# Windowed attention and a squared-ReLU feed-forward net in one kernel: attention re-tiled into chunks of 128 tokens

## Chip, cores, metric

One core of one Trainium2 chip. The time is device microseconds (us) of the whole launch, the median of several runs. All runs that are compared here are in the fast state (but for one single look, whose state is unknown), and each kernel was timed beside runs of the kernel before on the same chip. TensorE multiplies matrices, DVE is VectorE, ACT is ScalarE, POOL is GpSimd, and SP is SyncE, which issues all DMAs here. PSUM is the memory that TensorE writes, in banks; SBUF is the working memory.

## The reference

```python
# q, k, v: (8 batches, 8 heads, 576 tokens, 64), float32, entries about 0.1
scores = q @ k.T / 8                        # per batch and head
mask = (i - j >= 0) & (i - j < 64)          # causal, the last 64 keys
attn = softmax(where(mask, scores, -1e9))
x = (attn @ v) as (8 * 576 = 4608 tokens, 8 * 64 = 512)
h = maximum(x @ w_in, 0)                    # w_in  512 x 2048
out = (h * h) @ w_out                       # w_out 2048 x 512, out 4608 x 512 float32
```

## The kernel before

The feed-forward net (FFN) runs over nine blocks of 512 tokens: an up projection with a squared ReLU (16 steps of four matmuls of 512 columns), then the down projection (64 such matmuls). One batch of attention, 576 tokens, is woven step by step into each block; it feeds a later block. Attention goes head pair by head pair. Q and K are loaded with six consecutive tokens on one partition (rows of 1,536 bytes), cast on POOL and transposed on TensorE. The transposes come out with tokens in the order (r, t), so the copy out of PSUM puts them back in token order, with a write step of six 2-byte elements, that is 12 bytes:

```python
RT = 6; PT = S // RT                         # 6 tokens on each of 96 partitions
def transposes(hp):                          # one head pair, all 576 tokens
    for (s16, dstT, nm) in ((q16s, qTs, "q"), (k16s, kTs, "k")):
        ps = ps_att.tile([P, RT, PT], FP16, ...)          # a PSUM bank for each
        for r in range(RT):
            nc.tensor.transpose(out=ps[:, r, :], in_=s16[hp][:, r, :, :], ...)
        dT = attw.tile([P, PT, RT], FP16, ...)
        if nm == "q":                                     # line 168
            nc.scalar.activation(out=dT[:].rearrange("p t r -> p r t"), in_=ps[:], func=AF.Copy, ...)
        else:                                             # line 171
            nc.vector.tensor_copy(out=dT[:].rearrange("p t r -> p r t"), in_=ps[:])
# ... cut: scores (line 181), values, to_xT, and four more steps for the last 64 tokens
for hp in range(HP):                         # order of the steps of one batch
    transposes(hp); scores(hp)
    if hp > 0: values(hp - 1); to_xT(hp - 1)
# ... cut. PSUM: 3 buffers for the up projection, 2 for down, 3 for attention
for g in range(NTB + 1):                     # weave: steps of all streams evenly mixed
    weave(ffn_up(g), ffn_out(g - 1), attention steps of batch g + 1, loads of batch g + 2)
```

The softmax here doesn't subtract the row's maximum and nothing guards it: scores larger than these inputs give would overflow.

## Time and profile before

| | before |
|---|---|
| median of 3 runs | 383.81 us (382.3 to 386.02) |
| span of the profiled run | 380.5 us |
| first squared ReLU of block 0, of block 1 | 46.1, 83.2 us |
| pitch of the steady blocks that hold attention | 37.4 us |
| pitch of a block without attention (7 to 8) | 27.6 us |

Three stretches differ: a start, until block 1; woven blocks; and FFN alone at the end, where TensorE runs at its rate. The pitch is the distance between the first squared ReLUs of neighbouring blocks. The view of the PSUM tile of the up projection (hps) shows them; each line gives durations in ns (shortest/median/longest), then the first and last start in us:

```profile
L293 ACT ACTIVATE hrelu<-hps x144: 590/598/847, 44.9 to 362.0; 128x512 f32<-128x512 f32 x144
L294 DVE SCALAR_TENSOR_TENSOR h_601<-hps,hrelu x16: 674/688/810, 46.1 to 72.9; 128x512 f16<-128x512 f32 x16
L294 DVE SCALAR_TENSOR_TENSOR h_1161<-hps,hrelu x16: 659/692/812, 83.2 to 120.1; 128x512 f16<-128x512 f32 x16
...
L294 DVE SCALAR_TENSOR_TENSOR h_2345<-hps,hrelu x16: 691/692/692, 160.9 to 194.9; 128x512 f16<-128x512 f32 x16
L294 DVE SCALAR_TENSOR_TENSOR h_2937<-hps,hrelu x16: 691/692/692, 198.3 to 232.3; 128x512 f16<-128x512 f32 x16
```

198.3 - 160.9 is the pitch of 37.4. The groups of instructions (count, then busy us and mean ns, then idle time before and who ended it) give the price of the copies. The first two write with a step of 12 bytes, the third contiguously:

```profile
L168 ACT ACTIVATE qT<-qT_ps 128x576 f16<-128x576 f16 x32 | 67.4, 2105 | 29.3 <-PE qT_ps L164 29.2
L171 DVE COPY kT<-kT_ps 128x576 f16<-128x576 f16 x32 | 66.7, 2086 | 14.4 <-PE kT_ps L164 13.7
...
L218 DVE COPY xT<-xt_ps 128x512 f16<-128x512 f16 x32 | 13.4, 418 | 3.1 <-PE xt_ps L216 3.1
```

The list of waits has one large entry for TensorE (total us, times, longest); PEld is the load of the stationary operand:

```profile
PEld L181 <- DVE kT L171: 40.1, 32, 3.2
```

These 40.1 us are not all lost, since TensorE still multiplies while its next weight load waits (in the timeline below the load at 198.13 had waited 0.95 us, the first matmul after it 0.46).

The timeline of one such wait in a steady block (start us, duration, engine and line):

```profile
195.53 0.42 PE L164 MATMUL kT_ps<-ident,k_2419 96*128 96x96 f16 x6
...
195.79 1.03 PE L288 MATMUL hps<-xT,w_in_sb 128*128 128x512 f16 x4
195.99 2.09 DVE L171 COPY kT<-kT_ps 128x576 f16<-128x576 f16 x1 [0.18 <-PE kT_ps L164]
...
196.65 1.03 PE L307 MATMUL ops<-w_out_sb,h_2345 128*128 128x512 f16 x4
...
198.13 0.29 PEld L181 LDWEIGHTS <-kT 64*128 64x128 f16 x16 [0.95 <-DVE kT L171]
```

The four matmuls that start at 196.65 take 0.86 us of TensorE's time and would let the next work start near 197.5; the scores start at 198.13, when the K copy has ended. So about 0.6 us is lost for each head pair.

### The profile page before, as it was taken

The page shows a single profiled execution, that of the slowest core. Times are in us where ns is not written, and L with a number is a line of the kernel's source. Part 1 is how long each engine was busy: PE and PEld are TensorE (multiplying, and loading weights), DVE is VectorE, ACT ScalarE, POOL GpSimd, SP SyncE. Part 2 cuts the span into 40 slices and gives each one's busy share as a digit, 9 for nine tenths or more (in the row PEclk, how much of TensorE's full clock was granted, in tenths as well). Part 3 has the DMA queues.
Part 4 walks back from the last instruction along what each step waited for, and adds up shares of the span by engine and source line. Part 5 has one row for each costly group of instructions (what it writes and reads, how often), then busy time and mean ns, then how long its engine had stood idle before and what let it go on. Part 6 is the DMA issues. An engine that isn't in the chain of part 4 may idle for free.

```text
span 380.5 us, 7267 instructions
## 1 busy us (share of the span) xinstructions
PE 327.2 (86%) x2848; PEld 160.5 (42%) x2848; DVE 255.4 (67%) x468; ACT 215.0 (56%) x309; POOL 118.6 (31%) x178
## 2 busy tenths in 40 slices
PE   1154797777799999999999999999999999999995
PEld 1033443433444444454445444444444444444442
DVE  2277877888887888787878777877787744343400
ACT  3334276869665766576567656764676434444421
POOL 6922373552474752822182217310100000000000
PEclk9999998999999999999999999999999999999999
DMA  9946894957796899974254222100000001001012
GB/s 189 262 132 197 212 246 124 218 159 219 186 254 182 170 239 183 211 189 120 90 150 129 90 91 74 45 30 29 28 29 29 28 29 49 36 28 56 29 55 83
DMA packets 60642, 46.61 MB, mean 122 GB/s; under 512 B 39616, under 2 KB 51904, under 8 KB 60608
## 3 DMA queue, kind: packets, MB, share of 16 engines
q1 hardware_dynamic: 60608, 46.15, 47.0%
q8 instruction: 22, 0.36, 0.4%
q14 instruction: 12, 0.10, 0.1%
HBM read 36.70 MB, written 9.44 MB: 121 GB/s over the span
## 4 chain that ended last, share of the span: by engine, by line
PE 60%; DVE 23%; ACT 6%; DMA 4%; issue 3%; POOL 2%; SPq 0%; ACTq 0%; POOLq 0%
PE ops L307 25%; PE hps L288 23%; DVE kT L171 15%; DMA ws<-in_moe_w_in_dram 3%; PE av L204 2%; ACT hrelu L293 2%; DVE x_sb L209 2%; PE xt_ps L216 2%; PE qT_ps L164 2%; PE kT_ps L164 2%; DMA v_st<-in_v_dram 1%; ACT w_out_sb L123 1%; ACT qT L168 1%; DVE h_601 L294 1%; DVE w_in_sb L110 1%
## 5 line engine op out<-in xcount | busy, mean ns | idle before, releaser
L288 PE MATMUL hps<-xT,w_in_sb 128*128 128x512 f16 x576 | 155.6, 392 | 1.4 <-DVE h_601 L294 1.3
L293 ACT ACTIVATE hrelu<-hps 128x512 f32<-128x512 f32 x144 | 91.0, 637 | 88.8 <-PE hps L288 59.8
L168 ACT ACTIVATE qT<-qT_ps 128x576 f16<-128x576 f16 x32 | 67.4, 2105 | 29.3 <-PE qT_ps L164 29.2
L171 DVE COPY kT<-kT_ps 128x576 f16<-128x576 f16 x32 | 66.7, 2086 | 14.4 <-PE kT_ps L164 13.7
L288 PEld LDWEIGHTS <-w_in_sb 128*128 128x128 f16 x576 | 50.1, 100 | 49.2 <-issue 5.7
L312 ACT ACTIVATE osb<-ops 128x512 f32<-128x512 f32 x36 | 21.4, 598 | 21.4 <-PE ops L307 21.4
L181 PEld LDWEIGHTS <-kT 64*128 64x128 f16 x512 | 10.1, 99 | 41.2 <-DVE kT L171 40.1
L209 DVE TENSOR_TENSOR x_sb<-av,rden 128x256 f16<-128x256 f32 x64 | 25.0, 419 | 0.3
L294 DVE SCALAR_TENSOR_TENSOR h_4658<-hps,hrelu 128x512 f16<-128x512 f32 x16 | 11.1, 692 | 16.7 <-ACT hrelu L293 16.7
L294 DVE SCALAR_TENSOR_TENSOR h_4867<-hps,hrelu 128x512 f16<-128x512 f32 x16 | 11.1, 692 | 16.6 <-ACT hrelu L293 16.6
L152 POOL CAST v_ev_108<-v_st 128x512 f16<-128x512 f32 (+1 forms) x20 | 12.4, 631 | 30.6 <-DMA v_st<-in_v_dram 20.8
L216 PE MATMUL xt_ps<-ident,x_sb 128*128 128x128 f16 x128 | 13.3, 230 | 9.9 <-DVE x_sb L209 9.9
L152 POOL CAST v_ev_107<-v_st 128x512 f16<-128x512 f32 (+1 forms) x20 | 12.3, 622 | 22.7 <-DMA v_st<-in_v_dram 14.1
L307 PE MATMUL ops<-w_out_sb,h_601 128*128 128x512 f16 x64 | 18.5, 379 | 0.1
L216 PEld LDWEIGHTS <-x_sb 128*128 128x128 f16 x128 | 9.6, 102 | 18.8 <-DVE x_sb L209 14.3
L307 PE MATMUL ops<-w_out_sb,h_2345 128*128 128x512 f16 x64 | 16.6, 379 | 0.0
L307 PE MATMUL ops<-w_out_sb,h_3529 128*128 128x512 f16 x64 | 16.6, 379 | 0.0
L307 PE MATMUL ops<-w_out_sb,h_1753 128*128 128x512 f16 x64 | 16.6, 379 | 0.0
L307 PE MATMUL ops<-w_out_sb,h_1161 128*128 128x512 f16 x64 | 16.6, 379 | 0.0
L307 PE MATMUL ops<-w_out_sb,h_2937 128*128 128x512 f16 x64 | 16.6, 379 | 0.0
L307 PE MATMUL ops<-w_out_sb,h_4121 128*128 128x512 f16 x64 | 16.4, 379 | 0.0
L307 PE MATMUL ops<-w_out_sb,h_4658 128*128 128x512 f16 x64 | 16.4, 379 | 0.0
(717 smaller groups left out, 529.7 us busy)
## 6 DMA issues: line engine op xcount, KB each, us to landing
q_st<-in_q_dram SPq DMA_DIRECT2D x32, 288.0 KB, 4.6
k_st<-in_k_dram SPq DMA_DIRECT2D x32, 288.0 KB, 4.8
out_dram<-osb SPq DMA_DIRECT2D x36, 256.0 KB, 2.0
v_st<-in_v_dram SPq DMA_DIRECT2D x32, 256.0 KB, 4.5
ws<-in_moe_w_in_dram SPq DMA_DIRECT2D x16, 256.0 KB, 4.2
v_st<-in_v_dram SPq DMA_DIRECT2D x8, 128.0 KB, 5.3
ws_628<-in_moe_w_out_dram SPq DMA_DIRECT2D x1, 256.0 KB, 8.7
ws_663<-in_moe_w_out_dram SPq DMA_DIRECT2D x1, 256.0 KB, 8.7
```

The costliest lines, as they stand in the source:

```text
L152: nc.gpsimd.tensor_copy(out=v_ev[0:n, c, :, 0:D], in_=st[0:n])
L164: nc.tensor.transpose(out=ps[:, r, :], in_=s16[hp][:, r, :, :], identity=ident[0:PT, 0:PT])
L168: nc.scalar.activation(out=dT[:].rearrange("p t r -> p r t"), in_=ps[:], func=AF.Copy, scale=1.0)
L171: nc.vector.tensor_copy(out=dT[:].rearrange("p t r -> p r t"), in_=ps[:])
L181: nc.tensor.matmul(sc[hh][:, j, :], kTs[hp][r0:r0 + 64, ks:ks + P], qTs[hp][r0:r0 + 64, j * 64:(j + 1) * 64], start=True, stop=True)
L209: nc.vector.tensor_tensor(out=x_sb[:, :, hh, :], in0=av[:, :, 0:D], in1=rden[:].to_broadcast([P, NC, D]), op=ALU.mult)
L216: nc.tensor.transpose(out=xt[:, c, :], in_=hold["x"][:, c, :, :], identity=ident[:])
L288: nc.tensor.matmul(hps[:], w_in_sb[:, c, f * P:(f + 1) * P], xT[:, c, g * 512:(g + 1) * 512], start=(c == 0), stop=(c == DMC - 1))
L293: nc.scalar.activation(out=hrelu[:], in_=hps[:], func=AF.Relu)
L294: nc.vector.scalar_tensor_tensor(out=h2s[g][:, f, :], in0=hps[:], scalar=0.0, in1=hrelu[:], op0=ALU.max, op1=ALU.mult)
L307: nc.tensor.matmul(hold["ps"][:], h2s[g][:, f, ts * P:(ts + 1) * P], w_out_sb[:, f, :], start=(f == 0), stop=(f == FFC - 1))
L312: nc.scalar.activation(out=osb[:], in_=hold["ps"][:], func=AF.Copy, scale=OUT_SCALE)
```

## The change

Attention is cut into 36 chunks of 128 tokens over all eight heads, four to an FFN block. q, k and v are loaded with one token on a partition (rows of 256 bytes), so the transposes come out in token order and all copies out of PSUM are contiguous. Four stages are run as a pipeline over chunks: the transposes of a chunk come before the scores of the one before it. There is no tail of 64 tokens. K and Q of a chunk now share one PSUM tile. The w_in casts move from DVE to ACT with four staging buffers instead of three; PSUM has two up-projection buffers instead of three, and four for attention. Not in the cut below: more buffers for the loads of q, k and v (15), other masks, and a weave in which each stream has a start and an end. "The new order" below means all of this together. The diff, cut to its core:

```diff
-            for (src, dst16, nm) in ((q, q16s, "q"), (k, k16s, "k")):
-                st = stage.tile([PT, 2, RT, D], FP32, ...)
-                    in_=src[b, 2 * hp:2 * hp + 2].rearrange("h (p r) d -> p h (r d)", r=RT))
+        for (src, nm) in ((k, "k"), (q, "q"), (v, "v")):
+            st = stage.tile([P, H, D], FP32, ...)
+                    out=st[:], in_=src[b0, :, 64 * j0:64 * j0 + P, :].rearrange("h p d -> p h d"))
 ... (a chunk that spans two batches takes two DMAs of 64 tokens)
-                nc.vector.tensor_copy(out=dT[:].rearrange("p t r -> p r t"), in_=ps[:])
+        ps = ps_att.tile([P, 2, HP, P], FP16, name="qkT_ps", tag="ps_a")     # K and Q
+        kT = attw.tile([P, HP, 192], FP16, ...)
+            nc.vector.tensor_copy(out=kT[:, :, 0:64], in_=kTs[i - 1][:, :, P:192])   # carry
+        nc.vector.tensor_copy(out=kT[:, :, 64:192], in_=ps[:, 0])
+        nc.scalar.activation(out=qT[:], in_=ps[:, 1], func=AF.Copy, scale=1.0)
+    def attention(g):
+        fns = (transposes, scores, values, to_xT)
+        for t in range(4 + len(fns) - 1):
+            for s, fn in enumerate(fns):
+                if 0 <= t - s < 4:
+                    steps.append(lambda fn=fn, i=4 * g + t - s: fn(i))
-    wst = ctx.enter_context(tc.tile_pool(name="wst", bufs=3))
+    wst = ctx.enter_context(tc.tile_pool(name="wst", bufs=4))
-    ps_up = ... bufs=3 ... ps_att = ... bufs=3
+    ps_up = ... bufs=2 ... ps_att = ... bufs=4
-            nc.vector.tensor_scalar(   # w_in cast
+            nc.scalar.activation(
```

More of the change, by code (lines that the diff above doesn't have):

```diff
@@ L18, in weave @@
     keyed = []
-    for s, steps in enumerate(streams):
+    for s, (steps, lo, hi) in enumerate(streams):
         n = len(steps)
         for i, step in enumerate(steps):
-            keyed.append(((i + 0.5) / n, s, i, step))
+            keyed.append((lo + (hi - lo) * (i + 0.5) / n, s, i, step))
     keyed.sort(key=lambda e: e[:3])
@@ L43 @@
     HP = H // 2
-    RT = 6
-    PT = S // RT
-    NBM = 8
-    NC = 4
-    T0 = NBM * 64
-    TAIL = S - T0
+    NCK = NT // P
+    NB = S // 64
     W_SCALE = 100.0
@@ L57 @@
     const = ctx.enter_context(tc.tile_pool(name="const", bufs=1))
-    wst = ctx.enter_context(tc.tile_pool(name="wst", bufs=3))
-    stage = ctx.enter_context(tc.tile_pool(name="stage", bufs=4))
-    vstage = ctx.enter_context(tc.tile_pool(name="vstage", bufs=5))
-    st16 = ctx.enter_context(tc.tile_pool(name="st16", bufs=3))
+    wst = ctx.enter_context(tc.tile_pool(name="wst", bufs=4))
+    stage = ctx.enter_context(tc.tile_pool(name="stage", bufs=15))
+    st16 = ctx.enter_context(tc.tile_pool(name="st16", bufs=8))
@@ L62 @@
     attw = ctx.enter_context(tc.tile_pool(name="attw", bufs=3))
     smallp = ctx.enter_context(tc.tile_pool(name="smallp", bufs=4))
+    xtp = ctx.enter_context(tc.tile_pool(name="xtp", bufs=3))
     h2pool = ctx.enter_context(tc.tile_pool(name="h2pool", bufs=2))
-    hrp = ctx.enter_context(tc.tile_pool(name="hrp", bufs=3))
-    opool = ctx.enter_context(tc.tile_pool(name="opool", bufs=3))
-    ps_up = ctx.enter_context(tc.tile_pool(name="ps_up", bufs=3, space=bass.MemoryType.PSUM))
+    hrp = ctx.enter_context(tc.tile_pool(name="hrp", bufs=4))
@@ L68 @@
+    opool = ctx.enter_context(tc.tile_pool(name="opool", bufs=4))
+    ps_up = ctx.enter_context(tc.tile_pool(name="ps_up", bufs=2, space=bass.MemoryType.PSUM))
     ps_out = ctx.enter_context(tc.tile_pool(name="ps_out", bufs=2, space=bass.MemoryType.PSUM))
-    ps_att = ctx.enter_context(tc.tile_pool(name="ps_att", bufs=3, space=bass.MemoryType.PSUM))
+    ps_att = ctx.enter_context(tc.tile_pool(name="ps_att", bufs=4, space=bass.MemoryType.PSUM))
     ident = const.tile([P, P], FP16, name="ident")
@@ L72, with make_mask @@
     make_identity(nc, ident[:])
-    mask = const.tile([P, NBM, 64], FP16, name="mask")
-    nc.gpsimd.memset(mask[:], BIG)
-    nc.gpsimd.affine_select(
-        out=mask[:, 0, :], in_=mask[:, 0, :], compare_op=ALU.is_ge,
-        fill=0.0, base=0, pattern=[[1, 64]], channel_multiplier=-1,
-    )
-    nc.gpsimd.affine_select(
-        out=mask[:, 1:NBM, :], in_=mask[:, 1:NBM, :], compare_op=ALU.is_ge,
-        fill=0.0, base=-1, pattern=[[0, NBM - 1], [-1, 64]], channel_multiplier=1,
-    )
-    nc.gpsimd.affine_select(
-        out=mask[:, 1:NBM, :], in_=mask[:, 1:NBM, :], compare_op=ALU.is_ge,
-        fill=0.0, base=64, pattern=[[0, NBM - 1], [1, 64]], channel_multiplier=-1,
-    )
+    def make_mask(name, first):
+        m = const.tile([P, HP, 2, 64], FP16, name=name)
+        nc.gpsimd.memset(m[:], BIG)
+        nc.gpsimd.affine_select(
+            out=m[:], in_=m[:], compare_op=ALU.is_ge, fill=0.0, base=-1,
+            pattern=[[0, HP], [0, 2], [-1, 64]], channel_multiplier=1,
+        )
+        nc.gpsimd.affine_select(
+            out=m[:], in_=m[:], compare_op=ALU.is_ge, fill=0.0, base=64,
+            pattern=[[0, HP], [0, 2], [1, 64]], channel_multiplier=-1,
+        )
+        if first is not None:
+            nc.gpsimd.memset(m[0:64, :, first, :], 0.0)
+        return m
@@ L92 @@
+    mask_first = make_mask("mask_first", 0)
     w_in_sb = const.tile([P, DMC, DFF], FP16, name="w_in_sb")
     w_out_sb = const.tile([P, FFC, DM], FP16, name="w_out_sb")
-    xT = const.tile([P, DMC, NT], FP16, name="xT")
-    NV = 2
-    v_evs = [const.tile([P, NC + 1, H, 66], FP16, name=f"v_ev{i}") for i in range(NV)]
-    v_ods = [const.tile([P, NC, H, 66], FP16, name=f"v_od{i}") for i in range(NV)]
+    NV = 8
+    v_evs = [const.tile([P, H, 66], FP16, name=f"v_ev{i}") for i in range(NV)]
@@ L98 @@
+    v_ods = [const.tile([P, H, 66], FP16, name=f"v_od{i}") for i in range(NV)]
     for i in range(NV):
-        nc.vector.memset(v_evs[i][:, :, :, 64:65], 1.0)
-        nc.vector.memset(v_ods[i][:, :, :, 64:65], 1.0)
+        nc.vector.memset(v_evs[i][:, :, 64:65], 1.0)
+        nc.vector.memset(v_ods[i][:, :, 64:65], 1.0)
+    nc.vector.memset(v_ods[0][0:64, :, 0:D], 0.0)
     def load_w_in():
@@ L109, in one @@
                                                       quar * FQ:(quar + 1) * FQ])
-            nc.vector.tensor_scalar(
+            nc.scalar.activation(
                 out=w_in_sb[:, c, quar * FQ:(quar + 1) * FQ],
-                in0=ws[:], scalar1=W_SCALE, scalar2=None, op0=ALU.mult)
+                in_=ws[:], func=AF.Copy, scale=W_SCALE)
         for quar in range(4):
@@ L125, in load_w_out @@
         return [lambda f=f: one(f) for f in range(FFC)]
-    def attention(b):
-        steps = []
-        q16s, k16s = [None] * HP, [None] * HP
-        qTs, kTs = [None] * HP, [None] * HP
-        v_ev, v_od = v_evs[b % NV], v_ods[b % NV]
-        tail = {}
-        def load_qk(hp):
-            for (src, dst16, nm) in ((q, q16s, "q"), (k, k16s, "k")):
-                st = stage.tile([PT, 2, RT, D], FP32, name=f"{nm}_st", tag=f"{nm}_st")
-                nc.sync.dma_start(
-                    out=st[:].rearrange("p h r d -> p h (r d)"),
-                    in_=src[b, 2 * hp:2 * hp + 2].rearrange("h (p r) d -> p h (r d)", r=RT))
-                d16 = st16.tile([PT, RT, 2, D], FP16, name=f"{nm}16", tag=f"{nm}16")
-                nc.gpsimd.tensor_copy(out=d16[:].rearrange("p r h d -> p h r d"), in_=st[:])
-                dst16[hp] = d16
-        def load_v():
-            for c in range(NC + 1):
-                n = P if c < NC else TAIL
-                st = vstage.tile([P, H, D], FP32, name="v_st", tag="v_st")
-                nc.sync.dma_start(
-                    out=st[0:n], in_=v[b, :, c * P:c * P + n, :].rearrange("h p d -> p h d"))
-                nc.gpsimd.tensor_copy(out=v_ev[0:n, c, :, 0:D], in_=st[0:n])
-                if c > 0:
-                    nc.gpsimd.tensor_copy(out=v_od[64:P, c - 1, :, 0:D],
-                                          in_=v_ev[0:64, c, :, 0:D])
-                if c < NC:
-                    nc.gpsimd.tensor_copy(out=v_od[0:64, c, :, 0:D],
-                                          in_=v_ev[64:P, c, :, 0:D])
-        def transposes(hp):
-            for (s16, dstT, nm) in ((q16s, qTs, "q"), (k16s, kTs, "k")):
-                ps = ps_att.tile([P, RT, PT], FP16, name=f"{nm}T_ps", tag="ps_a")
-                for r in range(RT):
-                    nc.tensor.transpose(out=ps[:, r, :], in_=s16[hp][:, r, :, :],
-                                        identity=ident[0:PT, 0:PT])
-                dT = attw.tile([P, PT, RT], FP16, name=f"{nm}T", tag=f"{nm}T", bufs=5)
-                if nm == "q":
-                    nc.scalar.activation(out=dT[:].rearrange("p t r -> p r t"), in_=ps[:],
-                                         func=AF.Copy, scale=1.0)
-                else:
-                    nc.vector.tensor_copy(out=dT[:].rearrange("p t r -> p r t"), in_=ps[:])
-                dstT[hp] = dT[:].rearrange("p t r -> p (t r)")
-        def scores(hp, pms):
-            sc = [ps_att.tile([P, NBM, 64], FP32, name=f"sc{hh}", tag="ps_a")
-                  for hh in range(2)]
-            for j in range(NBM):
-                ks = 0 if j == 0 else 64 * (j - 1)
@@ new lines, with xT_of, load @@
+    xTs = {}
+    def xT_of(g):
+        if g not in xTs:
+            xTs[g] = xtp.tile([P, DMC, 512], FP16, name="xT", tag="xT")
+        return xTs[g]
+    q16s, k16s, qTs, kTs, pms, xs = {}, {}, {}, {}, {}, {}
+    def load(i):
+        sts = []
+        for (src, nm) in ((k, "k"), (q, "q"), (v, "v")):
+            st = stage.tile([P, H, D], FP32, name=f"{nm}_st", tag="st")
+            b0, j0 = divmod(2 * i, NB)
+            if j0 + 1 < NB:
+                nc.sync.dma_start(
+                    out=st[:], in_=src[b0, :, 64 * j0:64 * j0 + P, :].rearrange("h p d -> p h d"))
+            else:
+                nc.sync.dma_start(
+                    out=st[0:64], in_=src[b0, :, 64 * j0:S, :].rearrange("h p d -> p h d"))
+                nc.sync.dma_start(
+                    out=st[64:P], in_=src[b0 + 1, :, 0:64, :].rearrange("h p d -> p h d"))
+            sts.append(st)
+        k16s[i] = st16.tile([P, H * D], FP16, name="k16", tag="k16")
+        nc.gpsimd.tensor_copy(out=k16s[i][:], in_=sts[0][:].rearrange("p h d -> p (h d)"))
+        q16s[i] = st16.tile([P, H * D], FP16, name="q16", tag="q16")
+        nc.gpsimd.tensor_copy(out=q16s[i][:], in_=sts[1][:].rearrange("p h d -> p (h d)"))
+        v_ev, v_od, v_next = v_evs[i % NV], v_ods[i % NV], v_ods[(i + 1) % NV]
+        nc.gpsimd.tensor_copy(out=v_ev[:, :, 0:D], in_=sts[2][:])
+        nc.gpsimd.tensor_copy(out=v_od[64:P, :, 0:D], in_=v_ev[0:64, :, 0:D])
+        if i + 1 < NCK:
+            nc.gpsimd.tensor_copy(out=v_next[0:64, :, 0:D], in_=v_ev[64:P, :, 0:D])
@@ new lines, in transposes @@
+    def transposes(i):
+        ps = ps_att.tile([P, 2, HP, P], FP16, name="qkT_ps", tag="ps_a")
+        for s, src in enumerate((k16s, q16s)):
+            for hp in range(HP):
+                nc.tensor.transpose(out=ps[:, s, hp, :], in_=src[i][:, hp * P:(hp + 1) * P],
+                                    identity=ident[:])
+        kT = attw.tile([P, HP, 192], FP16, name="kT", tag="kT")
+        if i > 0:
+            nc.vector.tensor_copy(out=kT[:, :, 0:64], in_=kTs[i - 1][:, :, P:192])
+        else:
+            nc.vector.memset(kT[:, :, 0:64], 0.0)
+        nc.vector.tensor_copy(out=kT[:, :, 64:192], in_=ps[:, 0])
+        qT = attw.tile([P, HP, P], FP16, name="qT", tag="qT")
+        nc.scalar.activation(out=qT[:], in_=ps[:, 1], func=AF.Copy, scale=1.0)
+        kTs[i], qTs[i] = kT, qT
@@ L179, in scores @@
+    def scores(i):
+        sc = [ps_att.tile([P, HP, 2, 64], FP32, name=f"sc{hh}", tag="ps_a") for hh in range(2)]
+        for hp in range(HP):
+            for blk in range(2):
                 for hh in range(2):
@@ L181, in scores @@
                     nc.tensor.matmul(
-                        sc[hh][:, j, :], kTs[hp][r0:r0 + 64, ks:ks + P],
-                        qTs[hp][r0:r0 + 64, j * 64:(j + 1) * 64], start=True, stop=True)
-            for hh in range(2):
-                pm = attw.tile([P, NBM, 64], FP16, name=f"pm{hh}", tag=f"pm{hh}")
-                nc.scalar.activation(out=pm[:], in_=sc[hh][:], func=AF.Exp,
-                                     scale=1.0 / float(D) ** 0.5)
-                nc.vector.tensor_tensor(out=pm[:], in0=pm[:], in1=mask[:], op=ALU.min)
-                pms[hh] = pm
@@ L191, in keys_of @@
-        def keys_of(j, h):
-            if j == 0:
-                return v_ev[:, 0, h, 0:65]
-            if j % 2 == 1:
-                return v_ev[:, (j - 1) // 2, h, 0:65]
-            return v_od[:, (j - 2) // 2, h, 0:65]
-        def values(hp, pms, hold):
-            x_sb = attw.tile([P, NC, 2, D], FP16, name="x_sb", tag="x_sb")
-            hold["x"] = x_sb
-            for hh in range(2):
-                av = ps_att.tile([P, NC, 66], FP32, name="av", tag="ps_a")
-                for j in range(NBM):
-                    nc.tensor.matmul(
-                        av[(j % 2) * 64:(j % 2 + 1) * 64, j // 2, 0:65],
-                        pms[hh][:, j, :], keys_of(j, 2 * hp + hh), start=True, stop=True)
-                rden = smallp.tile([P, NC, 1], FP32, name="rden", tag="rden")
-                nc.vector.reciprocal(out=rden[:], in_=av[:, :, 64:65])
-                nc.vector.tensor_tensor(
-                    out=x_sb[:, :, hh, :], in0=av[:, :, 0:D],
-                    in1=rden[:].to_broadcast([P, NC, D]), op=ALU.mult)
@@ L213, in to_xT @@
-        def to_xT(hp, hold):
-            xt = ps_att.tile([P, NC, P], FP16, name="xt_ps", tag="ps_a")
-            for c in range(NC):
-                nc.tensor.transpose(out=xt[:, c, :], in_=hold["x"][:, c, :, :],
-                                    identity=ident[:])
-            nc.vector.tensor_copy(out=xT[:, hp, b * S:b * S + T0],
-                                  in_=xt[:].rearrange("p c t -> p (c t)"))
-        def tail_scores():
-            sc = [ps_att.tile([P, HP, 64], FP32, name=f"sct{hh}", tag="ps_a")
-                  for hh in range(2)]
-            for hp in range(HP):
-                for hh in range(2):
-                    r0 = 64 * hh
-                    nc.tensor.matmul(
-                        sc[hh][:, hp, :], kTs[hp][r0:r0 + 64, S - P:S],
-                        qTs[hp][r0:r0 + 64, T0:S], start=True, stop=True)
-            tail["pm"] = []
-            for hh in range(2):
-                pm = attw.tile([P, HP, 64], FP16, name=f"pmt{hh}", tag=f"pmt{hh}", bufs=2)
-                nc.scalar.activation(out=pm[:], in_=sc[hh][:], func=AF.Exp,
-                                     scale=1.0 / float(D) ** 0.5)
-                nc.vector.tensor_tensor(out=pm[:], in0=pm[:], in1=mask[:, 1:1 + HP, :],
-                                        op=ALU.min)
-                tail["pm"].append(pm)
@@ L239, in tail_values @@
-        def tail_values():
-            av = ps_att.tile([P, HP, 66], FP32, name="avt", tag="ps_a")
-            for hp in range(HP):
-                for hh in range(2):
-                    nc.tensor.matmul(
-                        av[hh * 64:(hh + 1) * 64, hp, 0:65], tail["pm"][hh][:, hp, :],
-                        v_od[:, NC - 1, 2 * hp + hh, 0:65], start=True, stop=True)
-            rden = smallp.tile([P, HP, 1], FP32, name="rdent", tag="rden")
-            nc.vector.reciprocal(out=rden[:], in_=av[:, :, 64:65])
-            x_t = attw.tile([64, HP, 2, D], FP16, name="x_t", tag="x_t", bufs=2)
-            for hh in range(2):
-                nc.vector.tensor_tensor(
-                    out=x_t[:, :, hh, :], in0=av[hh * 64:(hh + 1) * 64, :, 0:D],
-                    in1=rden[hh * 64:(hh + 1) * 64].to_broadcast([64, HP, D]), op=ALU.mult)
-            tail["x"] = x_t
@@ L255, in tail_to_xT @@
-        def tail_to_xT():
-            xt = ps_att.tile([P, HP, 64], FP16, name="xtt_ps", tag="ps_a")
-            for hp in range(HP):
-                nc.tensor.transpose(out=xt[:, hp, :], in_=tail["x"][:, hp, :, :],
-                                    identity=ident[0:64, 0:64])
-            nc.vector.tensor_copy(out=xT[:, :, b * S + T0:(b + 1) * S], in_=xt[:])
-        loads = [lambda hp=hp: load_qk(hp) for hp in range(HP)]
-        loads.insert(1, load_v)
-        pms = [[None, None] for _ in range(HP)]
@@ L265, in attention @@
-        holds = [{} for _ in range(HP)]
-        for hp in range(HP):
-            steps.append(lambda hp=hp: transposes(hp))
-            steps.append(lambda hp=hp: scores(hp, pms[hp]))
-            if hp > 0:
-                steps.append(lambda hp=hp - 1: values(hp, pms[hp], holds[hp]))
-                steps.append(lambda hp=hp - 1: to_xT(hp, holds[hp]))
-        steps.append(tail_scores)
-        steps.append(lambda: values(HP - 1, pms[HP - 1], holds[HP - 1]))
-        steps.append(lambda: to_xT(HP - 1, holds[HP - 1]))
@@ L275, in attention @@
-        steps.append(tail_values)
-        steps.append(tail_to_xT)
-        return loads, steps
+                        sc[hh][:, hp, blk, :], kTs[i][r0:r0 + 64, hp, 64 * blk:64 * blk + P],
+                        qTs[i][r0:r0 + 64, hp, 64 * blk:64 * blk + 64], start=True, stop=True)
+        j0 = 2 * i % NB
+        mask = mask_first if j0 == 0 else mask_second if j0 + 1 == NB else mask_inner
+        pms[i] = []
+        for hh in range(2):
+            pm = attw.tile([P, HP, 2, 64], FP16, name=f"pm{hh}", tag=f"pm{hh}")
+            nc.scalar.activation(out=pm[:], in_=sc[hh][:], func=AF.Exp,
+                                 scale=1.0 / float(D) ** 0.5)
+            nc.vector.tensor_tensor(out=pm[:], in0=pm[:], in1=mask[:], op=ALU.min)
+            pms[i].append(pm)
@@ new lines, in values @@
+    def values(i):
+        x_sb = attw.tile([P, H, D], FP16, name="x_sb", tag="x_sb")
+        for half in range(2):
+            av = ps_att.tile([P, 4, 66], FP32, name="av", tag="ps_a")
+            for h in range(4 * half, 4 * half + 4):
+                for blk in range(2):
+                    vv = (v_ods if blk == 0 else v_evs)[i % NV]
+                    nc.tensor.matmul(
+                        av[64 * blk:64 * blk + 64, h % 4, 0:65],
+                        pms[i][h % 2][:, h // 2, blk, :], vv[:, h, 0:65], start=True, stop=True)
+            rden = smallp.tile([P, 4, 1], FP32, name="rden", tag="rden")
+            nc.vector.reciprocal(out=rden[:], in_=av[:, :, 64:65])
+            nc.vector.tensor_tensor(
+                out=x_sb[:, 4 * half:4 * half + 4, :], in0=av[:, :, 0:D],
+                in1=rden[:].to_broadcast([P, 4, D]), op=ALU.mult)
+        xs[i] = x_sb
@@ new lines, in to_xT @@
+    def to_xT(i):
+        xt = ps_att.tile([P, DMC, P], FP16, name="xt_ps", tag="ps_a")
+        for c in range(DMC):
+            nc.tensor.transpose(out=xt[:, c, :], in_=xs[i][:, 2 * c:2 * c + 2, :],
+                                identity=ident[:])
+        nc.vector.tensor_copy(out=xT_of(i // 4)[:, :, (i % 4) * P:(i % 4 + 1) * P], in_=xt[:])
+    def attention(g):
+        steps = []
+        fns = (transposes, scores, values, to_xT)
[3 more added lines that the diff above has]
+                    steps.append(lambda fn=fn, i=4 * g + t - s: fn(i))
+        return steps
@@ L280, with loads @@
+    def loads(g):
+        return [lambda i=i: load(i) for i in range(4 * g, 4 * g + 4)]
     h2s = {}
@@ L288, in one @@
                 nc.tensor.matmul(
-                    hps[:], w_in_sb[:, c, f * P:(f + 1) * P],
-                    xT[:, c, g * 512:(g + 1) * 512],
+                    hps[:], w_in_sb[:, c, f * P:(f + 1) * P], xT_of(g)[:, c, :],
                     start=(c == 0), stop=(c == DMC - 1))
@@ L317, in ffn_out @@
         return [lambda ts=ts, fq=fq: one(ts, fq) for ts in range(4) for fq in range(4)]
-    loads, steps = attention(0)
-    for s in loads:
-        s()
-    w_in_steps = load_w_in()
-    for s in weave(steps, w_in_steps):
-        s()
-    nxt = attention(1)
-    for s in nxt[0]:
+    for s in loads(0):
+        s()
+    mask_inner = make_mask("mask_inner", None)
+    mask_second = make_mask("mask_second", 1)
+    for s in weave((attention(0), 0.0, 1.0), (load_w_in(), 0.0, 1.0)):
+        s()
+    for s in loads(1):
         s()
-    w_out_steps = load_w_out()
     for g in range(NTB + 1):
         streams = []
+        if g > 0:
+            streams.append((ffn_out(g - 1), 0.0, 1.0))
         if g < NTB:
-            streams.append(ffn_up(g))
-        if g > 0:
-            streams.append(ffn_out(g - 1))
-        if g + 1 < B:
-            streams.append(nxt[1])
-        if g == 0:
-            streams.append(w_out_steps)
-        if g + 2 < B:
-            nxt = attention(g + 2)
-            streams.append(nxt[0])
+            streams.append((ffn_up(g), 0.0, 1.0))
+        if g == 0:
+            streams.append((load_w_out(), 0.0, 0.6))
+        if g + 1 < NTB:
+            streams.append((attention(g + 1), 0.0, 0.95))
+        if g + 2 < NTB:
+            streams.append((loads(g + 2), 0.6 if g == 0 else 0.0, 1.0))
         for s in weave(*streams):
```

## The prediction

> **What bounds the kernel now.** Span 380.5 us, three regimes (first and last squared ReLU of each token block, view of the hps tile):
>
> - 0 to 83 us, start: first ReLU at 44.9 us, block 1 begins at 83.2. DMA moves about 190 GB/s; TensorE is busy under half until 40 us.
> - 83 to 309: blocks 1 to 6, each woven with one attention batch; steady pitch 37.4 us.
> - 309 to 380: FFN alone, 27.6 us a block, a 512-column matmul every 0.215 us: TensorE at its rate.
>
> A steady block is 27.6 FFN + 9.8 attention. From the timeline, TensorE's work for one head pair is 0.52 (transposes) + 0.44 (scores) + 0.47 (values) + 0.23 (transpose back); a batch with its tail about 6.9 us. The other 3 us are stalls: scores stand behind the K copy, whose strided write takes 2.09 us (DVE, 32 times; ACT pays 2.11 for Q). The waits list gives 40.1 us of weight loads behind kT; the chain of waits gives kT 15% of the span. The contiguous xT copy (512 elements, also from PSUM) takes 0.42 us. The Trainium skill, "SBUF — State Buffer", Door 1, says that each access crossing to a new 16-byte line pays a penalty; 2-byte writes 12 B apart against contiguous ones here, 3.6 against 0.8 ns per element, agree.
>
> **What the change does.**
> - K and Q copies: 66.7 us of DVE become 36 x (0.42 + about 0.15 carry), some 20; 67.4 us of ACT become 36 x 0.6 = 22. Nearly all off the path; what counts is that scores no longer wait.
> - TensorE attention per block: 4 x (8 x 0.055 + 0.44 + 0.47 + 0.23) = 6.3 us (estimate); nine blocks 57 us against 55: no gain in work.
> - The first FFN block needs 512 tokens, not 576, and no tail. w_in casts move from DVE (0.45) to ACT (0.6).
> - Cost: q and k go from 1,536 B to 256 B packets: 110,592 packets x 21.9 ns over 16 engines is 151 us against 123. Streams of 256 B packets reached 217 GB/s here, 1,536 B ones about 250. The skill, "DMA: Bandwidth & Descriptors", Specifications, puts full rate at 512 B and up; the trace agrees, mildly. Later, 3.1 MB per 34 us is easy.
> - FFN-up PSUM drops from 3 to 2 buffers; ReLU 0.64 + product 0.69 fit in some 3 us between uses.
>
> **Sum.** Start: q, k, v of group 0 (3.1 MB), w_in (4.2), group 1 (3.1), w_out (4.2) at about 205 GB/s: block 1 begins near 75 us, first ReLU near 33. Then 7 blocks at 27.6 + 6.3 = 33.9: 237; one at 27.2, the last 17.5. Span 357; the timed median stands some 3 us above the span before too: **359 us**, range **348 to 372**. Of the 25 us, about 17 come from stalls in woven blocks, 8 from the start. Chances: faster by over 2% 0.91, within 2% 0.08, slower 0.01.
>
> **What would show it.** kT waits nearly gone from list and chain; pitch 33 to 35 us; DVE busy about 220 us, ACT about 185; first ReLU at 30 to 36 us; packets under 512 B above 110,000, DMA share about 60%; 512-column matmuls unchanged.
>
> **What would make it wrong.** Small packets slowing the start (issuing a 1,024-row load took about 1 us on the queue); in-order issues holding loads behind output stores; two FFN-up buffers making TensorE wait for the product; GpSimd copies (3.1 us a chunk, now to the end) slowing DVE copies. Better: a start shorter than the DMA estimate.

## More of the kernel before

The matmuls of the scores themselves wait for kT for 23.3 us, summed over the whole list.

The chain of work that ended last (shares of the span) agrees that K copies matter:

```profile
PE 60%; DVE 23%; ACT 6%; DMA 4%; issue 3%; POOL 2%; SPq 0%; ACTq 0%; POOLq 0%
PE ops L307 25%; PE hps L288 23%; DVE kT L171 15%; DMA ws<-in_moe_w_in_dram 3%; PE av L204 2%; ACT hrelu L293 2%; DVE x_sb L209 2%; PE xt_ps L216 2%; PE qT_ps L164 2%; PE kT_ps L164 2%; DMA v_st<-in_v_dram 1%; ACT w_out_sb L123 1%; ACT qT L168 1%; DVE h_601 L294 1%; DVE w_in_sb L110 1%
```

In the start the same copies stand in the chain in order of time (start us, us, what):

```profile
17.93 2.08 DVE kT L171
...
33.90 2.08 DVE kT L171
...
49.26 1.99 DVE kT L171
...
59.10 1.98 DVE kT L171
...
67.17 2.09 DVE kT L171
```

## The result, and the profile after

The kernel after takes 352.46 us (350.75 to 353.53, 4 runs) against 383.31 us of the kernel before in the same rounds: ratio 0.918, 95% interval 0.912 to 0.924. Ratios are the mean time of one kernel's fast runs over that of the other's of the same rounds, so not quite the ratio of the medians quoted. The span of the profiled run is 351.8 us.

| | before | after | predicted |
|---|---|---|---|
| first squared ReLU of block 1, us | 83.2 | 70.0 | 75 |
| from there to that of block 8, us | 253.5 | 239.0 | 237 |
| from there to the end, us | 43.8 | 42.9 | 44.7 |
| steady pitch, us | 37.4 | 34.0 | 33.9 |
| DVE, ACT busy, us | 255, 215 | 202, 181 | 220, 185 |

The view of the up projection's tile:

```profile
L247 ACT ACTIVATE hrelu<-hps x144: 578/597/615, 31.0 to 334.2; 128x512 f32<-128x512 f32 x144
L248 DVE SCALAR_TENSOR_TENSOR h_580<-hps,hrelu x16: 675/692/692, 31.6 to 54.7; 128x512 f16<-128x512 f32 x16
L248 DVE SCALAR_TENSOR_TENSOR h_1086<-hps,hrelu x16: 675/691/693, 70.0 to 103.0; 128x512 f16<-128x512 f32 x16
...
L248 DVE SCALAR_TENSOR_TENSOR h_2706<-hps,hrelu x16: 664/692/694, 173.5 to 205.3; 128x512 f16<-128x512 f32 x16
L248 DVE SCALAR_TENSOR_TENSOR h_3244<-hps,hrelu x16: 681/692/694, 207.5 to 239.3; 128x512 f16<-128x512 f32 x16
```

The copies among the groups; L170 is the carry of 64 keys:

```profile
L175 ACT ACTIVATE qT<-qkT_ps 128x512 f16<-128x512 f16 x36 | 21.5, 596 | 19.7 <-DVE kT L173 19.7
L173 DVE COPY kT<-qkT_ps 128x512 f16<-128x512 f16 x36 | 15.2, 422 | 26.1 <-PE qkT_ps L166 26.1
...
L170 DVE COPY kT<-kT 128x256 f16<-128x256 f16 x35 | 11.4, 325 | 0.2
```

The wait for kT is almost gone:

```profile
PEld L184 <- DVE kT L173: 1.3, 1, 1.3
```

The waits of the scores for qT sum to 2.7 us.

And the chain of work that ended last is now TensorE:

```profile
PE 82%; DMA 5%; DVE 4%; POOL 4%; ACT 2%; issue 1%; SPq 1%; ACTq 0%; POOLq 0%
PE ops L261 36%; PE hps L243 33%; PE av L204 4%; PE qkT_ps L166 4%; DMA k_st<-in_k_dram 3%; PE xt_ps L217 2%; DMA ws<-in_moe_w_in_dram 2%; ACT hrelu L247 1%; DVE h_580 L248 1%; DVE x_sb L209 1%; SPq L144 1%; DVE kT L173 1%; ACT qT L175 1%; DVE h_1086 L248 0%; DVE rden L208 0%
```

The 28.7 us between the two spans are 13.2 from the start, 14.5 from the blocks and 0.9 from the end. The prediction had 8 from the start and 17 from the blocks. The pitches of the two kernels are not quite like for like: a woven block of the kernel before holds 576 tokens of attention, one of the kernel after 512. Between block 1 and block 8 the kernel before has six woven blocks and one without attention, the kernel after seven woven ones, so the sum from block 1 to block 8 is the fairer figure. Two questions follow. Is it the short copies that gain, or the new order of the steps? And why did the start gain more than foreseen?

### The profile page after: what moved, and what is told of

It reads as the page before. It is cut to its first block, busy times and chain, and to the rows that moved or that the text cites. A ratio compares the mean times of both kernels' runs of the same rounds, so it can differ in the third digit from the quotient of the medians.

```text
span 351.8 us, 7118 instructions
## 1 busy us (share of the span) xinstructions
PE 322.0 (92%) x2736; PEld 161.3 (46%) x2736; DVE 202.0 (57%) x485; ACT 180.9 (51%) x321; POOL 118.3 (34%) x196
## 4 chain that ended last, share of the span: by engine, by line
PE 82%; DMA 5%; DVE 4%; POOL 4%; ACT 2%; issue 1%; SPq 1%; ACTq 0%; POOLq 0%
PE ops L261 36%; PE hps L243 33%; PE av L204 4%; PE qkT_ps L166 4%; DMA k_st<-in_k_dram 3%; PE xt_ps L217 2%; DMA ws<-in_moe_w_in_dram 2%; ACT hrelu L247 1%; DVE h_580 L248 1%; DVE x_sb L209 1%; SPq L144 1%; DVE kT L173 1%; ACT qT L175 1%; DVE h_1086 L248 0%; DVE rden L208 0%
## 5 line engine op out<-in xcount | busy, mean ns | idle before, releaser
L243 PE MATMUL hps<-xT,w_in_sb 128*128 128x512 f16 x576 | 152.0, 385 | 5.6 <-DVE h_580 L248 4.7
L247 ACT ACTIVATE hrelu<-hps 128x512 f32<-128x512 f32 x144 | 85.8, 597 | 110.2 <-PE hps L243 109.4
L243 PEld LDWEIGHTS <-w_in_sb 128*128 128x128 f16 x576 | 56.5, 99 | 73.9 <-issue 10.3
L175 ACT ACTIVATE qT<-qkT_ps 128x512 f16<-128x512 f16 x36 | 21.5, 596 | 19.7 <-DVE kT L173 19.7
L173 DVE COPY kT<-qkT_ps 128x512 f16<-128x512 f16 x36 | 15.2, 422 | 26.1 <-PE qkT_ps L166 26.1
L209 DVE TENSOR_TENSOR x_sb<-av,rden 128x256 f16<-128x256 f32 x72 | 27.7, 415 | 0.3
L219 DVE COPY xT<-xt_ps 128x512 f16<-128x512 f16 x36 | 15.1, 420 | 15.3 <-PE xt_ps L217 15.3
L208 DVE RECIPROCAL rden<-av 128x4 f32<-128x4 f32 x72 | 11.9, 180 | 16.7 <-PE av L204 16.5
L248 DVE SCALAR_TENSOR_TENSOR h_4808<-hps,hrelu 128x512 f16<-128x512 f32 x16 | 11.1, 692 | 16.6 <-ACT hrelu L247 16.6
L248 DVE SCALAR_TENSOR_TENSOR h_580<-hps,hrelu 128x512 f16<-128x512 f32 x16 | 11.0, 690 | 13.1 <-ACT hrelu L247 13.1
L248 DVE SCALAR_TENSOR_TENSOR h_1086<-hps,hrelu 128x512 f16<-128x512 f32 x16 | 11.0, 688 | 9.1 <-ACT hrelu L247 9.1
L217 PE MATMUL xt_ps<-ident,x_sb 128*128 128x128 f16 x144 | 15.8, 236 | 0.3 <-DVE x_sb L209 0.3
```

Source lines behind the costliest of these rows:

```text
L173: nc.vector.tensor_copy(out=kT[:, :, 64:192], in_=ps[:, 0])
L175: nc.scalar.activation(out=qT[:], in_=ps[:, 1], func=AF.Copy, scale=1.0)
L209: nc.vector.tensor_tensor(out=x_sb[:, 4 * half:4 * half + 4, :], in0=av[:, :, 0:D], in1=rden[:].to_broadcast([P, 4, D]), op=ALU.mult)
L217: nc.tensor.transpose(out=xt[:, c, :], in_=xs[i][:, 2 * c:2 * c + 2, :], identity=ident[:])
L219: nc.vector.tensor_copy(out=xT_of(i // 4)[:, :, (i % 4) * P:(i % 4 + 1) * P], in_=xt[:])
L243: nc.tensor.matmul(hps[:], w_in_sb[:, c, f * P:(f + 1) * P], xT_of(g)[:, c, :], start=(c == 0), stop=(c == DMC - 1))
```

## The experiments

Twelve runs. One caution for all of them: the build orders each engine's instructions itself, so an edit also moves instructions. In b_contig, for one, the source line of TensorE's work differs from the kernel before at 117 of 2,848 places in order of start, though the edit touches copies alone. The block times of the experiments are read from the instructions' times in their traces, as in the table above: "block 1" is the first squared ReLU of block 1.

### 1. Short copies alone, in the kernel before (b_contig, b_kcontig)

```diff
-  out=dT[:].rearrange("p t r -> p r t")
+  out=dT[:].rearrange("p t r -> p (t r)").rearrange("p (r t) -> p r t", r=RT)
```

Both copies become contiguous, or K's alone. The columns are then in a wrong token order; nothing else changes. (The comparison with the reference passes all the same. The scores have a standard deviation of about 0.01 with these inputs, so the softmax weights hardly depend on them. These are not correct kernels, only measurements.)

> The kernel before, with the Q and K copies out of PSUM written contiguously; the token order of the copies is then wrong, so the result is wrong on purpose, the work is the same. Theory A (the length of the strided copies is what stalls TensorE): both copies drop from 2.1 us to about 0.45 (DVE) and 0.65 (ACT), the steady pitch from 37.4 to 34.5 us, the time from 383 to 358-366 us, because the copies also stand in the chain of the start. Theory B (the gain of the woven blocks comes from the re-tiled order, which puts other work between transposes and scores, and the gain of the start from fewer tokens to load): copies short, but pitch 36 us or more and time above 375.

Measured: 358.9 us, ratio 0.935 (0.929 to 0.942); block 1 at 71.3 us, steady pitch 35.3. The copies of b_contig among its groups:

```profile
L168 ACT ACTIVATE qT<-qT_ps 128x576 f16<-128x576 f16 x32 | 20.9, 652 | 28.2 <-PE qT_ps L164 28.2
L171 DVE COPY kT<-kT_ps 128x576 f16<-128x576 f16 x32 | 14.6, 456 | 17.9 <-PE kT_ps L164 17.4
```

The same 576 elements take 0.46 us instead of 2.09. That alone gives 24.5 of the 31 us, and 11.9 of the 13.2 us of the start (83.2 to 71.3). Theory A's time is met in the old order; the pitch of 35.3 is between the two forecasts. Of the 1.3 us by which this pitch exceeds the 34.0 of the kernel after, some 0.9 are the 64 more tokens in a block (an estimate: a ninth of 35.3 less 27.6).

> The kernel before with the K copy alone (DVE) contiguous; token order of K wrong on purpose, Q as before. b_contig gained 24.5 us with both. If the K copy is the wait, as the waits list named it (40.1 us behind kT, Q's copy runs beside it on ACT): 358-364 us. If both copies end at about the same time, so that the slower of the two holds the scores: scores wait for qT in its place, pitch stays above 36.5 us and the time above 372.

Measured: 371.77 us, ratio 0.974 (0.964 to 0.983), pitch 36.4, just under what the second forecast asked. By the medians that is about half of b_contig's gain; the interval spans the 2% line, and the profiled run, the slowest of the four, gained 8.0 us of b_contig's 25.5. With K short, scores wait for Q instead, as this wait of b_kcontig shows:

```profile
PE sc L181 <- ACT qT L168: 12.3, 30, 1.4
```

So the list of waits before named the later of two equal copies. Both had to go; the wait that the list shows was half of the story.

### 2. Long copies in the new order (a_slow, a repeat, a_slow_psum3, a_slow_split)

```diff
-        nc.vector.tensor_copy(out=kT[:, :, 64:192], in_=ps[:, 0])
+        jk = attw.tile([P, P, 6], FP16, name="jk", tag="jk")
+        nc.vector.tensor_copy(out=jk[:, :, 0:3].rearrange("p t r -> p r t"), in_=ps[:, 0, 0:3])
+        nc.vector.tensor_copy(out=kT[:, 0:3, 64:192], in_=jk[:, :, 0:3].rearrange("p t r -> p r t"))
+        nc.vector.tensor_copy(out=kT[:, 3, 64:192], in_=ps[:, 0, 3])
 ... (the same for Q on ACT, through jq)
```

> The kernel after, with each Q and K copy made as slow as before: three quarters of it go through a scratch tile with a write stride of 12 bytes, about 2.1 us in all, result right. Theory A (copy length): scores wait for kT again, pitch back from 34.0 to 36.5 us or more, time 368-378. Theory B (order): the other work between transposes and scores hides the copy, pitch at most 34.7, time at most 359.

Measured: 402.83 us, ratio 1.050 (1.044 to 1.056), steady pitches of 38.1 to 40.2: slower than the kernel before, which neither theory had. The K pieces sum to about 2.23 us, Q's to 2.66; the strided piece of each, which takes three quarters of the elements:

```profile
L180 ACT ACTIVATE jq<-qkT_ps 128x384 f16<-128x384 f16 x36 | 52.4, 1456 | 54.5 <-DVE kT L177 48.6 <-PE ops L270 5.8
L174 DVE COPY jk<-qkT_ps 128x384 f16<-128x384 f16 x36 | 51.8, 1439 | 13.8 <-PE qkT_ps L166 13.5
```

A second run of the same kernel, on the chip on which a_slow_split ran (its label says up3 by mistake; the kernel is a_slow unchanged), gave 403.77 us in a single look.

> The same kernel as a_slow once more, to see whether its 402.8 us and its pitch of 38 to 40 us stand on another chip; no theory differs here. Expected 398-407 us.

The first suspect was the up projection's two PSUM buffers. This run has three, with three for attention:

```diff
-    ps_up ... bufs=2    ps_att ... bufs=4
+    ps_up ... bufs=3    ps_att ... bufs=3
```

> a_slow (402.8) with PSUM split as in the kernel before, three FFN-up buffers and three for attention, instead of two and four, result right. a_slow came out slower than the kernel before, though its copies are about as long; its trace has TensorE wait 21.7 us for the squared ReLU to free an FFN-up buffer. If the two FFN-up buffers are why: 380-388 us. If the long copies hold up ACT and DVE themselves, whatever the buffers: above 396.

Measured: 415.64 us, ratio 1.084. The run does not clear that suspect by itself: the split also took a buffer from attention, and the granted TensorE clock was lower (0.942 against 0.973 in a_slow). The last run of this group does, since it keeps two buffers and is fast. The list of waits of a_slow held the next one: Q's copy starts only when K's has ended.

```profile
ACT jq L180 <- DVE kT L177: 48.6, 27, 3.4
```

K and Q share a PSUM tile of one bank in the new kernel. The Trainium skill, "PSUM — Partial Sum Buffer", section "PSUM bank collisions raise a hardware error", says that two engines must not touch the same bank and quadrant at once, reads included, and that software has to order them. Here the program makes ACT wait for DVE (whether because of the shared bank or of the shared tile, no run separates); in the kernel after the same wait is 19.7 us before qT, at no cost with copies of 0.42 us. The last run separates the two tiles:

```diff
-        ps = ps_att.tile([P, 2, HP, P], FP16, name="qkT_ps", tag="ps_a")
+        pss = [ps_att.tile([P, HP, P], FP16, name=f"{n}T_ps", tag="ps_a") for n in "kq"]
```

> a_slow (402.8) with K's and Q's transposes in two PSUM tiles, so in two banks, result right. In the kernel after both share one tile, and ACT's Q copy waits for DVE's K copy to end (48.6 us before jq in a_slow, 19.7 us before qT in the kernel after). If the two long copies in a row, 4.8 us, are why a_slow is slower than the kernel before: 372-386 us, and no wait of jq for DVE. If not, the order of the re-tiled kernel itself tolerates long copies worse: above 395.

Measured: 363.82 us, ratio 0.952 (0.945 to 0.959), better than either forecast. In its list of waits, jq now waits for TensorE only:

```profile
ACT jq L180 <- PE qT_ps L166: 16.8, 10, 4.5
```

From block 3 to block 7 its pitch is 33.9 to 34.1 us, that of the kernel after with short copies. Activity from 160 to 300 us (columns as in experiment 5: after the length comes TensorE's busy time) shows what the shared tile did, first of a_slow, then of a_slow_split:

```profile
160.00:300.00 140.00, 122.45 (x1068) 59.87 (x1067) 97.06 (x209) 84.96 (x144) 49.19 (x79) 1.00 0.53 114
```

```profile
160.00:300.00 140.00, 140.00 (x1256) 69.87 (x1256) 113.68 (x247) 97.03 (x168) 45.20 (x72) 1.00 0.48 109
```

So in the steady blocks the new order hides copies of over 2 us completely, as long as they run side by side: theory B holds there. Long copies still cost in the start: block 1 comes at 75.8 instead of 70.0 us, and the next pitch is 40.1 instead of 35.1.

The two theories are thus not rivals. Short copies in the old order are worth 24.5 us, the new order with long copies in two banks about 20 (383.8 to 363.8), and both together 31. Either of them removes most of the stall, so the shares cannot be added.

### 3. Rows of 256 bytes (a_bigpkt, b_contig_bigv)

```diff
-                out=st[:], in_=src[b0, :, 64 * j0:64 * j0 + P, :].rearrange("h p d -> p h d"))
 ... (and the two half loads)
+                out=st[:].rearrange("p h d -> p (h d)"),
+                in_=src.rearrange("b h s d -> (b h s) d")[i * 1024:(i + 1) * 1024, :]
+                .rearrange("(p h) d -> p (h d)", p=P))
```

> The kernel after, with q, k and v loaded as 2,048-byte rows of the flat tensors instead of 256-byte rows: same bytes, same issues, other tokens, so the result is wrong on purpose. If small packets cost time in the start (the prediction's cost of some 28 us of summed packet time, of which the start holds a quarter): first ReLU of block 1 falls from 70 to 64-67 us and the time by 3 to 6 us. If the start is bound by bytes alone: within 1 us. Steady pitch unchanged at 34.0 in both.

Measured: 342.93 us (wrong result), ratio 0.893 against 0.918 of the kernel after: 9.5 us by the medians, more than forecast. It also issues 108 loads where the kernel after issues 120, since no chunk is split. Block 1 comes at 63.3 us instead of 70.0, the blocks from 1 to 8 take 235.2 instead of 239.0, and the steady pitch is 34.0. So rows of 256 bytes, against rows of 2,048, cost 6.7 us before block 1 and 3.8 in the next blocks, nothing later. The profile does not say that all of the 6.7 is waiting for rows. Before block 1 TensorE ran at half its clock for 10.2 us in the kernel after, for 3.4 us in a_bigpkt (mean granted clock 0.93 and 0.97 below, third figure from the end). By an estimate from these stretches, 6.8 us more at half clock cost at most 3.4 us. Whether the small rows brought that about is not shown.

```profile
0.00:70.00 70.00, 44.95 (x439) 24.52 (x440) 35.49 (x107) 36.76 (x66) 32.08 (x58) 0.93 0.83 191
```

```profile
0.00:63.30 63.30, 45.36 (x463) 25.78 (x464) 38.05 (x111) 41.49 (x76) 37.63 (x68) 0.97 0.85 279
```

Neither kernel loads q and k in rows of 2,048 bytes. What the old rows of 1,536 bytes reach is seen at 12 to 14 us of the kernel before, where they are loaded alone (the last two figures are DMA share and GB/s):

```profile
12.00:14.00 2.00, 0.00 (x0) 0.00 (x0) 0.00 (x0) 0.00 (x0) 1.87 (x4) 1.00 1.12 250
```

The counterpart, on top of b_contig:

```diff
-                    out=st[0:n], in_=v[b, :, c * P:c * P + n, :].rearrange("h p d -> p h d"))
+                    out=st[0:n].rearrange("p h d -> p (h d)"),
+                    in_=v.rearrange("b h s d -> (b h s) d")[(b * S + c * P) * H:(b * S + c * P + n) * H, :]
+                    .rearrange("(p h) d -> p (h d)", p=n))
```

> b_contig with v also loaded as 2,048-byte rows, wrong result on purpose: so no load of q, k or v is under 1,536 bytes, as in a_bigpkt, and the two differ by the re-tiling alone. If the re-tiling by itself gains and the small packets took most of it back: at least 353 us, 10 us or more above a_bigpkt (342.9). If the re-tiling is worth nothing beyond the short copies: within 4 us of a_bigpkt.

This is the kernel before with short copies and v in rows of 2,048 bytes (wrong result). Measured: 355.47 us, ratio 0.932. It is 12.5 us above a_bigpkt: what the re-tiling, with all else in the change, is worth beyond short copies when no row is small (q and k have rows of 1,536 bytes here, 2,048 there). By the spans 6.6 lie before block 1, 5.0 in the blocks and 1.2 at the end. The kernel after gives about 9.5 of that back for its small rows, and b_contig pays 3.4 for its small rows of v (358.9 against 355.5), so the two differ by 6.4 us.

### 4. The w_in casts (a_win_dve)

```diff
-            nc.scalar.activation(out=w_in_sb[...], in_=ws[:], func=AF.Copy, scale=W_SCALE)
+            nc.vector.tensor_scalar(out=w_in_sb[...], in0=ws[:], scalar1=W_SCALE, ...)   # and wst bufs 4 -> 3
```

> The kernel after, with the w_in casts back on DVE and three weight buffers instead of four. If this part of the change made the start shorter: first ReLU from 31.6 to 36-40 us and time 3 to 6 us longer. If the start gained from short copies and fewer tokens alone: first ReLU within 1.5 us of 31.6, time within 1.5 us of the kernel after.

Measured: 354.93 us, ratio 0.924 (0.919 to 0.929), first squared ReLU at 33.9 us, block 1 at 70.6. The 2.5 us lie between the forecasts, and the intervals overlap: not settled, but a small matter.

### 5. Trying for a faster kernel (a_wst16, c_wout_first, c_lag2_wst8)

The DMAs of the kernel after have a hole: the weight loads wait for one of four staging buffers, which ACT frees late, since its casts stand behind attention in the order. The first candidate has 16 buffers:

```diff
-    wst = ctx.enter_context(tc.tile_pool(name="wst", bufs=4))
+    wst = ctx.enter_context(tc.tile_pool(name="wst", bufs=16))
```

> The kernel after with 16 weight staging buffers instead of 4, result right. In its trace DMA falls to 9 GB/s at 20-24 us and to 111 and 81 GB/s at 56-64 us, where weight loads wait on SyncE's queue for a cast on ACT to free a buffer. If those holes cost time: first ReLU of block 1 from 70 to 62-66 us, time 345-349. If the start is bound elsewhere (packets, TensorE's order): at most 2 us.

Measured: 348.38 us (348.2 to 348.91), ratio 0.912 (0.904 to 0.920), result right; the time is in the first forecast, block 1 (below) is not. It beats the kernel after by 4 us, or 1.2%; the runs of the two do not overlap, but they are from different chips and the intervals of the ratios do overlap. Activity by windows (window, length, then busy us of TensorE, its weight loads, DVE, ACT and POOL, granted clock, DMA share, GB/s), first of the kernel after, then of a_wst16:

```profile
10.00:15.00 5.00, 2.17 (x40) 1.59 (x40) 2.21 (x4) 1.57 (x3) 4.77 (x8) 1.00 1.28 218
20.00:25.00 5.00, 4.10 (x76) 3.15 (x77) 2.67 (x10) 2.72 (x6) 3.11 (x6) 1.00 0.02 7
```

```profile
10.00:15.00 5.00, 2.44 (x48) 1.80 (x48) 2.21 (x4) 1.67 (x4) 4.83 (x9) 1.00 1.33 218
20.00:25.00 5.00, 4.31 (x78) 3.40 (x79) 2.90 (x11) 2.99 (x6) 2.85 (x6) 1.00 1.02 379
```

At 10 to 15 us rows of 256 bytes are loaded, at 218 GB/s; at 20 to 25 us a_wst16 loads weights in rows of 2,048 bytes, at 379 GB/s, where the kernel after nearly stops. Block 1 comes at 67.0 us; a_wst16 gained 3.0 us there and 1.8 in the blocks up to block 8.

The second adds to it the w_out loads before those of group 1:

```diff
+    for s in load_w_out():
+        s()
     for s in loads(1):
         s()
-            streams.append((load_w_out(), 0.0, 0.6))      # in block 0
-            streams.append((loads(g + 2), 0.6 if g == 0 else 0.0, 1.0))
+            streams.append((loads(g + 2), 0.0, 1.0))
```

> A version meant to beat both: a_wst16 (348.4) with the w_out loads issued before the q, k, v loads of group 1, result right. In a_wst16 TensorE waits for group 1's chunks (12.6 us behind the K casts) and then runs attention of group 1 alone from 50 to 59 us; with w_out there first, the down projection of block 0 can fill that. If the start is held by the order of loads: 340-345 us. If the sum of bytes and packets before block 1 holds it whatever their order: 347-349.

Measured: 350.19 us, ratio 0.913 (0.910 to 0.917): no gain over a_wst16, and slower than both forecasts. Block 1 comes later (78.8 us) and the blocks up to block 8 take 227.2 us instead of 237.2: the work was only moved.

The third runs the down projection two blocks late, with 8 buffers:

```diff
-    for g in range(NTB + 1):
-        if g > 0:
-            streams.append((ffn_out(g - 1), 0.0, 1.0))
+    for g in range(NTB + 2):
+        if g > 1:
+            streams.append((ffn_out(g - 2), 0.0, 1.0))
 ... (w_out loads in block 1, h2 bufs 2 -> 3, wst bufs 4 -> 8)
```

> The other order: the kernel after with 8 weight buffers, the down projection two blocks behind the up projection instead of one, w_out loaded last, result right. If TensorE's idle time in the start is a lack of ready work: 341-346 us. If a longer pipeline only moves the idle time to its end: 347-352.

Measured: 353.92 us, ratio 0.924, slower than both forecasts and no better than the kernel after. Block 8 starts 13.6 us earlier than in the kernel after (295.4 against 309.0), but the end grew from 42.9 to 56.7 us, by one down projection of 13.8. The longer pipeline moved TensorE's idle time and did not fill it. What would fill it stays open.

## Why the prediction was right, and where its sum was off

The measured 352.46 us lies in the range, and the sign and the cause of the gain were right. Point by point:

- **Steady blocks: right.** Predicted 33.9 us, measured 34.0. The estimate of 6.3 us of TensorE's work for attention in a block fits: 34.0 less 27.6 is 6.4. The waits for kT fell from 40.1 to 1.3 us. Experiments 1 and 2 show that the short copies and the new order each achieve most of this.
- **"Of the 25 us, about 17 come from stalls in woven blocks, 8 from the start": the split was off.** Measured 14.5 and 13.2. The step that failed is the reading of the start as a matter of bytes ("at about 205 GB/s: block 1 begins near 75 us"), while the copies were called "nearly all off the path" but for the scores. Contiguous copies alone, with the old loads, moved block 1 from 83.2 to 71.3 us. The start before was a chain through 2 us copies nearly as much as through loads: of its first 84 us the chain that ended last spends 12.3 on K copies and 17.0 on loads of w_in and v. In the predicted span the start was 5 us too long and the blocks 2 us too short; that these partly cancelled was luck.
- **Small rows: the comparison was right for the old rows, but it left out better ones.** The prediction compared 217 GB/s with "about 250" and called the loss mild. The 250 stands (12 to 14 us of the kernel before, experiment 3). But rows of 2,048 bytes moved at 379 GB/s in a_wst16, and against such rows a_bigpkt puts the loss at 9.5 us. The Trainium skill, "DMA: Bandwidth & Descriptors", Specifications, asks for 512 bytes and more for full rate. The runs agree that 256 bytes are too few; but rows of 1,536 bytes did not reach the rate of 2,048 here. They also land on 96 partitions and not 128, and no run separates the two.
- **Busy times.** ACT was right (181 against 185). DVE fell to 202, not 220: of the terms in the text, the K copies' 46.7 and the w_in casts' 7.3 come off 255.4, so 220 was a slip of the sum. The carry took 0.325 us, about twice the estimate of 0.15, at no visible cost.
- **Offset.** The median of the kernel after lies 0.7 us above its profiled span, not 3. The predicted span of 357 against 351.8 gives 5.2 of the miss of 6.5 us, this the rest.
- **Not foreseen:** K and Q in one PSUM bank, which costs nothing visible with short copies and about 39 us with long ones (402.8 against 363.8, on different chips).

## What to carry to other kernels

When a wait names one copy, look for its twin on another engine, which may end at the same time, and check whether the two run side by side or through one PSUM bank. A long copy can be made short or hidden behind the next chunk's work; each alone brings most of the gain, so their values do not add up. Judge row sizes of loads in the stretch that is bound by loads, and compare their rate with that of the longest rows in the trace too, not only with that of the rows they replace.

## What the Trainium skill lacked or had wrong

- "SBUF — State Buffer", Door 1, gives the rule of 16-byte lines, at least two hits for each, but no size of the loss on DVE or ACT. Here the same 576 2-byte elements out of PSUM took 2.09 us on DVE with a write step of 12 bytes and 0.46 contiguously, on ACT 2.10 and 0.65.
- "DMA: Bandwidth & Descriptors", section "Bandwidth", has its measured table for DMAs issued from GpSimd and by size alone; it explains why small descriptors are slow, but without a measured rate by row size. Here loads of 256 KB issued from SyncE ran at 218 GB/s with rows of 256 bytes and at 379 GB/s with rows of 2,048 bytes; loads of 288 KB with rows of 1,536 bytes onto 96 partitions ran at 250 GB/s.
- "PSUM — Partial Sum Buffer" explains that engines must take turns on a bank, but not what it does to a schedule: 48.6 us of waits and 39 us of time in a_slow against a_slow_split.
- "TensorE: Matmul & The Clock Gate" warns of idle gaps of about 3 us; it also names short idle times between groups of matmuls as a cause, without saying how short or how many. In the kernel after the granted clock fell to half for 6.8 us (59.1 to 65.9) although TensorE had been busy 65% of the 3.4 us before, with no gap there above 0.6 us, on attention's small matmuls and transposes alone. The gap before that was 1.8 us (53.7 to 55.5). What set the clock down is not shown. These are the two windows of the kernel after, the stretch before and the stretch itself:

```profile
55.70:59.10 3.40, 2.21 (x63) 1.66 (x55) 2.37 (x9) 2.08 (x4) 1.83 (x3) 1.00 0.44 162
59.10:65.90 6.80, 6.26 (x67) 3.62 (x66) 4.89 (x17) 5.07 (x10) 0.15 (x1) 0.50 0.53 116
```
